# One second-stage matmul ahead of each convolution burst, and another order of the convolution's PSUM banks

## The chip, the cores and the metric

The kernel runs on one core of a Trainium2 chip. The metric is the device time of one execution in microseconds (us); lower is better. A core has a matrix engine (TensorE, PE in the profile, with PEld for its weight loads), a vector engine (VectorE, DVE), a scalar engine (ScalarE, ACT), GpSimd (POOL) and SyncE (SP), which here issues most DMAs. The engines run side by side and meet through semaphores. Matmul sums land in PSUM[...].

## The reference

Two steps follow each other. The first is a causal convolution over 7 positions with softmax weights, one set for each of 8 heads of 24 channels. The second is a feed-forward layer whose hidden value is the largest of three products.

```python
def _attn_ref(x, weight):                  # x: 8 x 4160 x 192, weight: 8 x 7
    w = softmax(weight, axis=-1)           # written out with exp and sum
    x_pad = np.concatenate([np.zeros((B, 6, D)), x], axis=1)
    idx = np.arange(S)[:, None] + np.arange(7)[None, :]
    x_unf = x_pad[:, idx, :].reshape(B, S, 7, 8, 24)
    return np.einsum('hk,bskhg->bshg', w, x_unf).reshape(B, S, D)

def _moe_ref(x, w1, w2, w3, w_out):        # x: 33280 x 192, w1..w3: 192 x 768, w_out: 768 x 192
    h = np.maximum(np.maximum(x @ w1, x @ w2), x @ w3)
    return h @ w_out
```

## The kernel before

**Blocks.** The 33280 tokens are cut into `NB` = 65 blocks of 512. Block t passes through three stages, in an order that the program writes out by hand: the loop `for t in range(2, NB)` issues, for each t, the first layer of block t, the second layer of block t-1, and in some turns the convolution of later blocks. Blocks 0 to 3 are convolved in another way (`conv_dense`) and play no part here.

**Convolution, a "burst".** `conv(u, pools)` (L301) issues 16 matmuls, 8 heads by two column halves, with 70 rows of `band` as weights. It writes tiles G into four PSUM banks, two heads each, and covers two blocks (u and u+1), except for block 4. It is issued right after `l1(t, 0)`: at t=3 for blocks 5 and 6, and at each even t from 4 to 60 for blocks t+3 and t+4. That makes 30 bursts of four banks; the one at t=2, for block 4 alone, uses two. `evac` (L347) copies a G bank to `ys`; `turn` (L358) and `double` (L366) then transpose and double it by DMAs from SP's queue into `yd`, the convolved block. `load_x` fetches x, and `cast_x` (L158) casts it on GpSimd.

**First layer.** `l1(t, j)` computes 128 of the 768 hidden values. The products are written as differences from the third: lp, for w1-w3, uses rows 0 to 63 of TensorE, the lower half; lq, for w2-w3, uses rows 64 to 127, the upper half. Each takes three matmuls of 512 columns, issued in turn, lp, lq, lp, lq, lp, lq (L399). ScalarE then makes `r` from lp (L403), and VectorE makes `h` from r and lq (L404). What was subtracted comes back in the second layer through the small matrix `m16`, which multiplies `yd`.

**Second layer.** `st2(t, u, NU)` issues one sixth of a block's second layer: five steps of two matmuls of 192 columns (L442), one in the lower half into tile po0 and one in the upper half into po1. The two halves keep sums of their own, and a pair of banks serves two of the block's four groups of 128 tokens. When both are complete, ScalarE copies po0 to `a` (L451), VectorE adds po1 to give `o` (L452), and `store` (L471) sends it out from GpSimd's queue.

**Order on TensorE.** For each j: six first-layer matmuls of block t, then ten second-layer matmuls of block t-1. At a burst, its 16 matmuls stand between `l1(t, 0)` and `st2(t-1, 0, NJ)`. This is the text of that stretch:

```python
        l1(t, 0)
        ...
        conv(u, PQ if t == 2 else WW + PQ)
        ...
        st2(t - 1, 0, NJ)
        for j in range(1, NJ):
            l1(t, j)
            st2(t - 1, j, NJ)
```

**PSUM banks.** Pool `psp` (tag p) has two banks for lp, `psq` (q) two for lq, and `psw` (w) four, which all po tiles share with two of a burst's G tiles. The other two G tiles take one bank of p and one of q. A pool hands out the bank that has been free longest, and the first matmul into it waits until the former tile has been read. As a burst takes one q bank, the lq of j=1 gets the bank of the lq of j=0, whose reader is h of j=0.

Of the kernel before, what the change touches and what calls it, by code (L numbers as in the profile page):

```python
# [27 lines left out]
def kernel(  # L28
# [19 lines left out]
    NJ = DFF // P  # L48
# [8 lines left out]
    for b in range(B):  # L57
        s = nfull * NBLK
        while s < SEQ:
            n = min(SEQ - s, NBLK - off)  # L60
# [8 lines left out]
    NB = len(blocks)  # L69
# [37 lines left out]
    psp = ctx.enter_context(tc.tile_pool(name="psp", bufs=2, space=bass.MemoryType.PSUM))  # L107
    psq = ctx.enter_context(tc.tile_pool(name="psq", bufs=2, space=bass.MemoryType.PSUM))
    psw = ctx.enter_context(tc.tile_pool(name="psw", bufs=4, space=bass.MemoryType.PSUM))
# [32 lines left out]
    def place(t):  # L142
        return (t, 0, 1) if t == NDENSE else (t - (t - NDENSE - 1) % 2, (t - NDENSE - 1) % 2, 2)
# [110 lines left out]
    def make_wd(j0, j1, eng=nc.vector):  # L254
        f = slice(P * j0, P * j1)
        eng.tensor_sub(out=wd[:, :, f], in0=ws[:, :, f], in1=w3s[:, :, f])  # L256
# [5 lines left out]
    def cast_w3(part):  # L262
        f = slice(PW * part, PW * (part + 1))
        nc.gpsimd.tensor_copy(out=w3h[:, :, f], in_=w3s[0:HALF, :, f])
# [24 lines left out]
    dense, hs, outs, halves, convs, done = {}, {}, {}, {}, {}, {}  # L289

    def conv(t, pools):
        if t >= NB:
            return
        t0, _, nu = place(t)
        n = len(pools)
        per = NHEAD // n
        w = nu * (NR // 2) * GRP
        G = [pool.tile([P, per, w], FP32, tag=tag, name=f"G{i}_{t}") for i, (pool, tag) in enumerate(pools)]
        for h in range(NHEAD):
            for c in range(2):  # L300
                nc.tensor.matmul(  # L301
                    G[h // per][HALF * c:HALF * (c + 1), h % per, :],
                    lhsT=band[0:HALF + PAD, h, PAD:HALF + PAD],
                    rhs=x16s[t0][0:HALF + PAD, h, c, :, :, :].rearrange("p u r c -> p (u r c)"),
                    start=True, stop=True, tile_position=(0, HALF * c))
        slots[t0] = ysp.tile([P, nu, NR // 2, D], FP16, tag="ys", name=f"ys_{t}")
        convs[t0] = G
# [75 lines left out]
    def y_tok(t, i, c, s):  # L383
        row = slice(HALF * i, HALF * (i + 1))
        if t < NDENSE:
            return dense[t][row, c, P * s:P * (s + 1)]
        k = spot(i, NC * s + c)
        return dense[t][row, k // (NCH // 2), k % (NCH // 2), :]
# [14 lines left out]
        nc.scalar.activation(out=r[:, 0:N], in_=ps[0][:, 0:N], func=AF.Relu)  # L403
        nc.vector.tensor_max(out=hs[t][:, j, 0:N], in0=r[:, 0:N], in1=ps[1][:, 0:N])  # L404

    def st2(t, u, NU):

        if t < 0:  # L410
            return
        hT = hs[t]
        if u == 0:
            todo = [[], []]
            for s in range(4):
                for i in range(2):
                    row = slice(HALF * i, HALF * (i + 1))
                    mm = [(y_tok(t, i, i, s), m16[row, 0, :])]
                    if s % 2 == i:
                        mm.append((y_tok(t, i, 2, s), m16[row, 1, :]))  # L420
                    hh = [(hT[row, j, P * s:P * (s + 1)], wo[row, j, :]) for j in range(NJ)]
                    mm = hh + mm if t == 0 else mm + hh
                    todo[i] += [(s, n == 0, n == len(mm) - 1, m) for n, m in enumerate(mm)]
            if t == NB - 1:

                for i in range(2):
                    k = [sum(e[0] < s for e in todo[i]) for s in range(5)]
                    lot = [todo[i][k[s]:k[s + 1]] for s in range(4)]
                    todo[i] = lot[0][:-1] + lot[1][:-1] + lot[0][-1:] + lot[1][-1:] + lot[2] + lot[3]
            halves[t] = (todo, {})  # L430
        todo, ps = halves[t]
        n = len(todo[0])
        for e in range(n * u // NU, n * (u + 1) // NU):
            for i in range(2):
                s, first, last, (a, b) = todo[i][e]
                b0 = s if t == NB - 1 else s - s % 2
                if (b0, i) not in ps:
                    pool, tag = (psw, "w")
                    if t == NB - 1 and s in (1, 2):
                        pool, tag = (psp, "p") if i == 0 else (psq, "q")  # L440
                    ps[b0, i] = pool.tile([P, 2, D], FP32, tag=tag, name=f"po{i}_{t}_{s}")
                nc.tensor.matmul(ps[b0, i][:, s % 2, :], lhsT=a, rhs=b, start=first, stop=last)  # L442
            ends = {todo[i][e][0] for i in range(2) if todo[i][e][2]}
            for s in sorted(ends):
                done[t, s] = done.get((t, s), 0) + sum(todo[i][e][0] == s and todo[i][e][2] for i in range(2))
                if done[t, s] < 2 or (s % 2 == 0 and t < NB - 1):
                    continue
                s0 = s if t == NB - 1 else s - 1
                ss = slice(s0 % 2, s % 2 + 1)
                a = tp.tile([P, 2, D], FP32, tag="a", name=f"a_{t}_{s}")  # L450
                nc.scalar.copy(out=a[:, ss, :], in_=ps[s0, 0][:, ss, :])  # L451
                nc.vector.tensor_add(out=outs[t][:, s0:s + 1, :], in0=a[:, ss, :],  # L452
                                     in1=ps[s0, 1][:, ss, :])
                if t == NB - 1 and s == 1:
                    store(t, 0, 2, (nc.sync,))
                elif t == NB - 1 and s == 3:
                    store(t, 2, 3, (nc.scalar,))
                    store(t, 3, 4, (nc.sync,))

    def store(t, s0, s1, qs):  # L460
        if t < 0:
            return
        ob, segs = outs[t], blocks[t]
        if len(segs) == 1:
            r = segs[0][0] * SEQ + segs[0][1] + P * s0
            todo = [(0, P, r, P)]
        else:
            assert all((b, S, n, off) == (b, SEQ - HALF, HALF, HALF * b) for b, S, n, off in segs)
            todo = [(HALF * i, HALF, (2 * s0 + i) * SEQ + SEQ - HALF, 2 * SEQ) for i in range(2)]
        for i, (p0, n, r, step) in enumerate(todo):  # L470
            qs[0].dma_start(out=bass.AP(tensor=out.tensor, offset=r * D,  # L471
                                        ap=[[D, n], [step * D, s1 - s0], [1, D]]),
                            in_=ob[p0:p0 + n, s0:s1, :])

    assert all(n == NBLK for n in blkN)
    def begin(t):
        hs[t] = hp.tile([P, NJ, NBLK], FP16, tag="h", name=f"h_{t}")
        outs[t] = outp.tile([P, 4, D], FP32, tag="o", name=f"o_{t}")


    PQ = ((psp, "p"), (psq, "q"))
    WW = ((psw, "w"), (psw, "w"))
    begin(0)
    begin(1)
    copy_w3(nc.vector.tensor_copy, 0)
# [16 lines left out]
    cast_w3(1)  # L502
    l1(1, 1, WW)
    transpose_w3(0)
# [4 lines left out]
    make_wd(4, 6, nc.gpsimd)  # L509
    l1(0, 3, WW)  # L510
    transpose_w3(2)
    l1(1, 2)
    l1(1, 3, WW)
    l1(0, 4)
    nc.gpsimd.tensor_copy(out=wo[:], in_=wos[:])
    l1(0, 5, WW)
    make_m(0)
# [17 lines left out]
    for t in range(2, NB):  # L535
        if t > 4:
            load_x(t + 6)
        for u in doubles_at.get(t, (t + 2,)):
            double(u)
        if t == 4:  # L540
            load_x(t + 6)
        if t > 3:
            cast_x(t + 5)
        begin(t)
        l1(t, 0)
        if t == 2:
            conv_dense(3, (nc.scalar.copy, nc.vector.tensor_copy, nc.scalar.copy))
            cross_dma(3)
            load_x(7)
        u = convs_at.get(t, t + 3 if t % 2 == 0 else NB)  # L550
        conv(u, PQ if t == 2 else WW + PQ)
        if t == 2:
            evac(u, 0)
            evac(u, 1, nc.vector.tensor_copy)
        else:
            for i in (0, 2):
                evac(u, i)
            for i in (3, 1):
                evac(u, i, nc.vector.tensor_copy)
        if t == 2:  # L560
            turn(4)
            load_x(8)
            cast_x(5)
            cast_x(6)
        elif t == 3:
            turn(5)
            turn(6)
            load_x(9)
            cast_x(7)
            cast_x(8)  # L570
        else:
            turn(t + 3)
# [4 lines that stand above are left out]
            if t == NB - 1 and j == 3:  # L577
                store(t - 1, 0, 2, (nc.sync,))
        if t == NB - 1:
            store(t - 1, 2, 4, (nc.sync,))  # L580
        else:
            store(t - 1, 0, 4, (nc.gpsimd,))
# [30 lines left out]
```

The softmax here doesn't subtract the row's maximum and nothing guards it: scores larger than these inputs give would overflow.

## Time and profile before

| what | value |
|---|---|
| median of 4 runs | 467.73 us (467.29 to 468.32) |
| the profiled execution | 467.5 us |
| its span in the profile | 465.7 us |
| TensorE busy, instructions | 459.9 us (99%), 7065 matmuls |
| VectorE, ScalarE, GpSimd busy | 359.0, 316.8, 162.5 us |
| one lp or lq matmul; one po; one G (mean as recorded) | 376, 243, about 250 ns |
| r; h; a; o (mean) | 597, 685, 471, 541 ns |

The span runs from the first to the last instruction that the profile shows; 1.8 us of the execution lie around it. A matmul's record has a start and a modelled end. Matmuls of one half follow each other more closely than the recorded durations, so the distance from start to start tells the pace. In the timeline each row gives the start and the duration in us, then engine, line, operation and tiles out<-in; "x16" means that 16 instructions are merged in the row. PEclk, the clock granted to TensorE, is full over the whole span.

### The profile page before, as it was taken

How to read it: one execution, taken by the hardware profiler on the slowest of the kernel's cores; microseconds unless marked ns; L12 is line 12 of the kernel's file. 1: busy time of each engine (PE TensorE's matmuls, PEld its weight loads, DVE VectorE, ACT ScalarE, POOL GpSimd, SP SyncE). 2: the span in 40 equal slices, each digit the busy share in tenths (PEclk: the TensorE clock that was granted, in tenths of full speed). 3: DMA queues.
4: the chain of work that ended last, by engine and by line, in shares of the span. 5: the costliest groups of instructions: out<-in, count | busy, mean ns of one | idle time of the engine just before them, and what ended most of it. 6: DMA issues, size and time to landing. Idle time of an engine off the chain costs nothing.

```text
span 465.7 us, 17191 instructions
## 1 busy us (share of the span) xinstructions
PE 459.9 (99%) x7065; PEld 386.1 (83%) x7065; DVE 359.0 (77%) x607; ACT 316.8 (68%) x609; POOL 162.5 (35%) x227
## 2 busy tenths in 40 slices
PE   8999999999999999999999999999999999999996
PEld 4587888888888888888888888988888898888996
DVE  6777877778777787787877777777778777777775
ACT  5766666666676766766667667676676666766664
POOL 5744434234324324433423432332343343243010
PEclk9999999999999999999999999999999999999999
DMA  8958997777678877979777867778686975794512
GB/s 199 236 133 203 207 230 170 170 202 168 182 187 167 185 183 178 177 170 208 186 138 202 170 186 181 191 166 182 180 173 165 210 191 146 187 164 108 118 69 103
DMA packets 107114, 81.14 MB, mean 174 GB/s; under 512 B 53110, under 2 KB 101980, under 8 KB 107036
## 3 DMA queue, kind: packets, MB, share of 16 engines
q1 hardware_dynamic: 99804, 55.17, 58.7%
q0 software_dynamic: 7072, 24.78, 14.8%
q8 instruction: 55, 0.90, 0.9%
q14 instruction: 23, 0.19, 0.1%
q10 hardware_dynamic: 160, 0.10, 0.1%
HBM read 30.28 MB, written 25.56 MB: 120 GB/s over the span
## 4 chain that ended last, share of the span: by engine, by line
PE 98%; DVE 0%; ACT 0%; issue 0%; DVEq 0%
PE lq L399 35%; PE po L442 33%; PE lp L399 22%; PE G L301 5%; PE idle L215 1%; PE D L319 1%; PE lw L399 0%; PE band_cols L239 0%; DVE wd L256 0%; PE pm L284 0%; PE pm L280 0%; ACT yd L328 0%; ACT yd L326 0%; ACT yd L325 0%; DVE h L404 0%
## 5 line engine op out<-in xcount | busy, mean ns | idle before, releaser
L404 DVE TENSOR_TENSOR h<-r,lq 128x512 f16<-128x512 f16 x386 | 264.6, 685 | 98.6 <-ACT r L403 98.5
L403 ACT ACTIVATE r<-lp 128x512 f16<-128x512 f32 x386 | 230.5, 597 | 136.8 <-PE lp L399 123.9
L399 PE MATMUL lp<-yd,wd 64*128 64x512 f16 x1158 | 312.1, 376 | 0.6 <-DVE wd L256 0.6
L399 PE MATMUL lq<-yd,wd 64*128 64x512 f16 x1158 | 312.2, 376 | 0.4 <-DVE yd L335 0.4
L442 PE MATMUL po<-wo,h 64*128 64x192 f16 x3120 | 249.0, 243 | 0.0
L442 PEld LDWEIGHTS <-h 64*128 64x128 f16 x3120 | 204.1, 94 | 16.8
L399 PEld LDWEIGHTS <-wd 64*128 64x128 f16 x2340 | 166.7, 94 | 28.0 <-issue 4.9
L471 POOL DMA_DIRECT2D out_dram<-o x64 | 48.1, 752 | 282.3 <-DVE o L452 215.9
L158 POOL CAST x<-xf 70x768 f16<-70x768 f32 x122 | 97.3, 832 | 3.3 <-DMA xf<-in_x_dram 2.9
L442 PE MATMUL po<-m,yd 64*128 64x192 f16 x780 | 95.8, 243 | 0.0
L452 DVE TENSOR_TENSOR o<-a,po 128x384 f32<-128x384 f32 (+1 forms) x132 | 71.3, 541 | 0.6 <-ACT a L451 0.6
L442 PEld LDWEIGHTS <-yd 64*128 64x128 f16 x780 | 58.0, 94 | 10.5
L451 ACT COPY a<-po 128x384 f32<-128x384 f32 (+1 forms) x132 | 62.0, 471 | 2.1 <-PE po L442 2.1
L347 DVE CAST ys<-G 128x384 f16<-128x384 f32 x61 | 31.0, 549 | 0.0
L301 PEld LDWEIGHTS <-band 70*64 70x64 f16 x496 | 19.5, 109 | 12.8 <-PE lp L399 12.7
L347 ACT CAST ys<-G 128x384 f16<-128x384 f32 x61 | 26.2, 486 | 0.0
L301 PE MATMUL G<-x,band 70*64 70x192 f16 (+1 forms) x496 | 26.1, 248 | 0.0
L215 PE MATMUL idle<-idle 128*128 128x512 f16 x15 | 6.3, 564 | 1.2 <-DVE idle L210 1.2
L177 POOL CAST xz<-xf 112x80 f16<-112x80 f32 (+2 forms) x18 | 5.2, 330 | 4.1 <-DMA xf<-in_x_dram 4.1
L319 PEld LDWEIGHTS <-xz 112*32 112x32 f16 x240 | 4.4, 105 | 1.9 <-DVE xz L177 0.8
L335 DVE COPY yd<-yd 64x512 f16<-64x512 f16 x9 | 4.2, 470 | 1.4 <-ACT yd L328 0.6
L319 PE MATMUL D<-band,xz 112*32 112x103 f16 (+1 forms) x240 | 5.0, 225 | 0.0
(45 smaller groups left out, 50.8 us busy)
## 6 DMA issues: line engine op xcount, KB each, us to landing
xf<-in_x_dram SPq DMA_DIRECT2D x57, 420.0 KB
out_dram<-o POOLq DMA_DIRECT2D x62, 384.0 KB, 3.7
yd<-yd SPq DMA_DIRECT2D x122, 96.0 KB
xf<-in_x_dram SPq DMA_DIRECT2D x7, 367.5 KB
ws<-in_moe_w_dram SPq DMA_DIRECT2D x6, 192.0 KB
yd<-ys SPq DMA_TRANSPOSE x61
w3s<-in_moe_w_dram SPq DMA_DIRECT2D x3, 192.0 KB
wos<-in_moe_w_out_dram SPq DMA_DIRECT2D x1, 576.0 KB
```

What stands on the lines that cost most here:

```text
L158: nc.gpsimd.tensor_copy(out=x16s[t0][0:K, :, c, u, :, :].rearrange("p h r c -> p r h c"), in_=xf[0:K, c:NR:2, :].rearrange("p r (h c) -> p ...
L215: nc.tensor.matmul(ps[:], lhsT=idle[:, 0:P], rhs=idle[:], start=True, stop=True)
L301: nc.tensor.matmul(G[h // per][HALF * c:HALF * (c + 1), h % per, :], lhsT=band[0:HALF + PAD, h, PAD:HALF + PAD], rhs=x16s[t0][0:HALF + PAD ...
L319: nc.tensor.matmul(ps[32 * g:32 * g + 32, lo:hi], lhsT=xz[t][v][0:rlen, q, 32 * s:32 * s + 32], rhs=band[0:rlen, h, cc:cc + hi - lo], star ...
L347: copy(out=slots[t][:, :, :, GRP * per * i:GRP * per * (i + 1)].rearrange("p u r (h c) -> p h (u r) c", c=GRP), in_=G[i][:].rearrange("p h ...
L399: nc.tensor.matmul(ps[i][:, 0:N], lhsT=wd[row, c, P * j:P * (j + 1)], rhs=y_all(t, i, c), start=(c == 0), stop=(c == NC - 1))
L403: nc.scalar.activation(out=r[:, 0:N], in_=ps[0][:, 0:N], func=AF.Relu)
L404: nc.vector.tensor_max(out=hs[t][:, j, 0:N], in0=r[:, 0:N], in1=ps[1][:, 0:N])
L442: nc.tensor.matmul(ps[b0, i][:, s % 2, :], lhsT=a, rhs=b, start=first, stop=last)
L451: nc.scalar.copy(out=a[:, ss, :], in_=ps[s0, 0][:, ss, :])
L452: nc.vector.tensor_add(out=outs[t][:, s0:s + 1, :], in0=a[:, ss, :], in1=ps[s0, 1][:, ss, :])
L471: qs[0].dma_start(out=bass.AP(tensor=out.tensor, offset=r * D, ap=[[D, n], [step * D, s1 - s0], [1, D]]), in_=ob[p0:p0 + n, s0:s1, :])
```

## The change

Ahead of each of the 30 bursts, one second-layer matmul is issued: the lower-half one of the first step of `st2(t-1, 0, NJ)`. It takes its po0 bank from `psw` before the burst takes its own. Behind the burst, `st2` leaves that one out (a set `ahead` remembers it), so the first second-layer matmul there is its upper-half partner; all others follow as before. The burst's four banks are filled in the order w, p, w, q instead of w, w, p, q. ScalarE evacuates the first w and then p, VectorE q and then the second w, as before; only the indices change.

```diff
-    def st2(t, u, NU):
+    ahead = set()
+
+    def st2(t, u, NU, first_half_only=False):
...
-        if u == 0:
+        if t not in halves:
...
-        for e in range(n * u // NU, n * (u + 1) // NU):
+        es = range(n * u // NU, n * (u + 1) // NU)
+        for e in es[:1] if first_half_only else es:
             for i in range(2):
+                if first_half_only:
+                    if i:
+                        break
+                    ahead.add((t, e))
+                elif i == 0 and (t, e) in ahead:
+                    continue
...
+    WPWQ = ((psw, "w"), (psp, "p"), (psw, "w"), (psq, "q"))
...
-        conv(u, PQ if t == 2 else WW + PQ)
+        if t > 2 and u < NB:
+            st2(t - 1, 0, NJ, True)
+        conv(u, PQ if t == 2 else WPWQ)
...
-            for i in (0, 2):
+            for i in (0, 1):
                 evac(u, i)
-            for i in (3, 1):
+            for i in (3, 2):
                 evac(u, i, nc.vector.tensor_copy)
```

## Prediction, made before the changed kernel was run

> **What bounds the kernel now.** The page first: one engine has no idle time, and the chain that ended last runs through it.
>
> ```profile
> PE 459.9 (99%) x7065; PEld 386.1 (83%) x7065; DVE 359.0 (77%) x607; ACT 316.8 (68%) x609; POOL 162.5 (35%) x227
> ...
> PE lq L399 35%; PE po L442 33%; PE lp L399 22%; PE G L301 5%; PE idle L215 1%; PE D L319 1%; PE lw L399 0%; PE band_cols L239 0%; DVE wd L256 0%; PE pm L284 0%; PE pm L280 0%; ACT yd L328 0%; ACT yd L326 0%; ACT yd L325 0%; DVE h L404 0%
> ```
>
> But TensorE is two streams: lp and the lower po run in rows 0 to 63, lq and the upper po in rows 64 to 127. "PE busy" hides a half that stands still while the other works, and so does the waits view, which lists no wait of a matmul on VectorE inside the loop. So I read next the timeline around a conv burst (G, L301), and took the starts to the nanosecond from the trace's records. First a burst that lq enters 0.10 us behind lp:
>
> ```profile
> 220.86 0.38 PE L399 MATMUL lp<-yd,wd 64*128 64x512 f16 x1
> 220.96 0.38 PE L399 MATMUL lq<-yd,wd 64*128 64x512 f16 x1
> ...
> 221.27 0.85 PE L301 MATMUL G<-x,band 70*64 70x192 f16 x16
> 221.28 0.60 ACT L403 ACTIVATE r<-lp 128x512 f16<-128x512 f32 x1
> 221.45 0.55 DVE L452 TENSOR_TENSOR o<-a,po 128x384 f32<-128x384 f32 x1
> ...
> 221.91 0.68 DVE L404 TENSOR_TENSOR h<-r,lq 128x512 f16<-128x512 f16 x1
> ...
> 222.05 0.34 PE L442 MATMUL po<-m,yd 64*128 64x192 f16 x3
> ...
> 222.48 0.38 PE L399 MATMUL lp<-yd,wd 64*128 64x512 f16 x1
> ...
> 222.65 0.37 PE L399 MATMUL lq<-yd,wd 64*128 64x512 f16 x1
> ```
>
> Then the burst before it, entered 0.17 us behind:
>
> ```profile
> 207.09 0.38 PE L399 MATMUL lp<-yd,wd 64*128 64x512 f16 x1
> 207.26 0.38 PE L399 MATMUL lq<-yd,wd 64*128 64x512 f16 x1
> 207.50 0.60 ACT L403 ACTIVATE r<-lp 128x512 f16<-128x512 f32 x1
> ...
> 207.57 0.85 PE L301 MATMUL G<-x,band 70*64 70x192 f16 x16
> ...
> 208.77 0.38 PE L399 MATMUL lp<-yd,wd 64*128 64x512 f16 x1
> 208.88 0.37 PE L399 MATMUL lq<-yd,wd 64*128 64x512 f16 x1
> ```
>
> Let Z be the start of the last lp matmul ahead of a burst and s the lag of lq behind lp. The 30 bursts from t=3 on agree within 4 ns: first G at Z+s+0.306; last G 0.605 later; first po 0.178 after that, so T = Z+s+1.089; five po per half (steps 0.093, then 0.0825), so lp of j=1 at T+0.424 = Z+s+1.513. The first lq of j=1 does not follow at once: it starts at **Z+1.785 in every burst, whatever s is**. Its bank is the one that h of j=0 reads. r starts at Z+0.413 and takes 0.597, h runs from Z+1.050 to Z+1.731, and lq follows 0.054 later. So on this path lq waits for lp, r, h, and the new lag is 1.785-1.513-s = 0.272-s. That is the alternation of the two fences: 0.098 gives 0.174, 0.172 gives 0.100 (the next group takes 0.003 off).
>
> From there to the next burst the upper half runs without a gap: 12.085 us in both kinds, eleven groups of 1.06 and the matmuls of the twelfth. One burst period is therefore (1.785-s)+12.085: **a larger lag on entering a burst is time saved, one for one**. The lags of the 29 bursts from t=4 on sum to 3.949, mean 0.136.
>
> **What the Trainium skill says.** "TensorE: Matmul & The Clock Gate", section "Back-to-back issue gap", gives N/2.4+2.5 ns: 215.8 for 512 columns and 82.5 for 192. The trace agrees: 0.216 between lp matmuls, 0.0825 between po. Its Part 3, "The mechanism", says that matmuls start and end strictly in program order. The trace disagrees between row halves: an lp starts at 220.432, ahead of the last po before it in the program, at 220.450. So the lower half may run ahead. "TensorEngine Tiling (Array Packing)", "Key Properties": a change of tiling mode drains the engine. The trace agrees: G starts 0.306 after the last lq, where the next matmul of that half would come after 0.216. "Perfetto Trace Analysis", "Tensor Engine Instruction", says matmul ends are modelled; I use starts only.
>
> **The change, part by part.** No instruction is added or removed. In 30 bursts (t=3 and every even t from 4 to 60) one lower po goes ahead of G, its upper partner stays first behind G.
>
> Ahead of G: the lower half is free at Z+0.216, and this po streams until Z+0.2985. The upper half streams until Z+s+0.216. With s above 0.083 the po lies under it and G does not move: cost nothing. It reads yd and m16, which are long there, not h; its bank's former sums, of the block before, were copied out some 3 us earlier.
>
> Behind G: the lower half has four po instead of five, so lp of j=1 comes at T+0.3415 = Z+s+1.431. lq stays at Z+1.785, since lp, r and h of j=0 do not move. The new lag is 0.354-s, less the 0.003: two lags in a row average 0.1755. Only half of the 0.0825 is gained, since the chain over r and h holds lq.
>
> Can the lag get that large? While lq waits, the weight load of the second lp is held behind it (in the first fence it is issued at 222.649, 2 ns after that lq). That lp is due 0.216 after the first, so about 0.21 is free. From 0.095 at t=3 the lags go 0.21, 0.14, 0.21: 15x0.21+14x0.1405 = 5.12. If they settle at once it is 29x0.1755 = 5.09. Gain 1.17 or 1.14 us.
>
> The end: the last block's po wait for h of its j=5, which follows from lp, not lq (the trace's lag falls to 0.005 at 460.58). lp is earlier than lq's gain says by the growth of the final lag, from 0.100 to 0.14 or 0.1755: 0.04 to 0.075 more. **Sum: 1.21 us.**
>
> The bank order w, p, w, q: nothing. ScalarE still copies the first w and then p; it has p's sums 0.165 earlier but is in the first copy (0.47 us). VectorE still takes q, then w, so the last evacuation stays, and with it the transposing DMA of SP behind it, the doubling DMAs, and POOL's stores and casts; none of these queues gets or loses an instruction. Waits that change place: the second G bank (p) waits for r of the block before (ended by Z-0.05, needed at Z+s+0.50); the third (w) for the copy a (ends Z+0.32, needed at Z+s+0.66); q as before. Covered also at s=0.095. The upper po now heads the queue behind G and waits for the add o (ends Z+1.134, seen 0.05 later: Z+1.184). With it late the lower po would stand behind it; it is in time when T is later, s above 0.095. At 0.14 the margin is 45 ns.
>
> Against its own time the profiled execution (467.5, span 465.7 and 1.8 around it) goes to 466.3. The median of four runs is 467.73, 0.2 above, so the forecast is 466.5.
>
> **Unknown costs.** (a) Where the drain is counted from, with a po as the last matmul ahead of G: from the end of both streams (G unmoved, which I take, since the trace counts it from the later half), or 0.306 after the po's own start, Z+0.522. (b) What a late weight load costs the second lp, c. Lower bound zero: the load at 222.649 was 0.043 ahead and cost nothing. Behind G loads come 4 ns ahead and the next step is 0.093 for 0.0825: c=0.01, which I take. Upper bound: the 0.094 that a load lasts. Earlier than due it cannot be, so no gain.
>
> **Rivals.** A, the drain follows the po: G at Z+0.522, lp of j=1 at Z+1.647, lag 0.1385 always, 0.135 at entry; 29x(0.136-0.135) is nothing, the tail gives 0.035: 467.7. For it: nothing here shows a short matmul ahead of G; against it: s+0.306 in both kinds.
> B, slower: the held weight load stalls the lower half at each burst. The lag is capped at 0.212-c; from c above 0.077 it falls under today's mean. The floor is 0.095 (at t=2 the lag is 0.003 on leaving and 0.095 six groups later), reached at c=0.12: 29x0.041 = 1.19 lost, 468.9. For it: the load is held in every burst; against it: the second lp came after 0.216 in all 30.
> C, the whole po is gained, 30x0.0825 = 2.5: 465.3. It needs lq free of h, and 1.785 in every burst speaks against it.
>
> **How the numbers follow.** About 0.2%, 0.94 us, is what a measurement here tells from no change. Main case 0.76 (own range 466.2 to 466.9), A 0.14, B 0.07, C 0.03. Faster by over 0.2%: 0.70 of the main case and C, 0.73; within 0.2%: 0.06 of the main case and A, 0.20; slower: B, 0.07. Range 466.0 to 467.8: it takes in the main case with the scatter of a median (runs 467.29 to 468.32) and A; B and C stay out.
>
> **What would show it.** Right: lq of j=1 still at Z+1.785; G at Z+s+0.306; lp of j=1 at Z+s+1.431; lags near 0.21 and 0.14 or all near 0.175; bursts 13.69 us apart on the mean (13.735 now). Wrong: lags of 0.1385 (A), under 0.13 with the second lp over 0.216 after the first (B), lq of j=1 before Z+1.7 (C), or a po that starts after the last lq has streamed.

## The result, and the profile after

The changed kernel takes **466.52 us** (median of 44 runs; 466.5 was forecast), the kernel before 467.76 us (median of 63). The ratio is 0.9968, 95% interval 0.9959 to 0.9977: faster, by about 0.3%. The ratio is one of means over the fast runs, so it leaves out two runs of the changed kernel, of 793 and 2650 us, and takes in nine runs of the kernel before near 471 us; the medians give 0.9973.

The page of the changed kernel shows almost none of it. Here are the busy times and the row of G's weight loads, whose last part is the idle time ahead of them (12.8 us before):

```profile
PE 459.4 (99%) x7065; PEld 370.9 (80%) x7065; DVE 359.1 (77%) x607; ACT 318.9 (69%) x609; POOL 162.6 (35%) x227
...
L301 PEld LDWEIGHTS <-band 70*64 70x64 f16 x496 | 19.5, 109 | 11.5 <-PE lp L399 11.4
```

TensorE's busy time is down by 0.5 us on the same 7065 matmuls, at 99% as before. The recorded time of the weight loads fell more, from 386.1; it goes with the lag of lq behind lp (400.1 us in e3 below, 357.0 in e4), and why it does is open. The span is only 0.7 us shorter, because in this execution the first of the 30 bursts comes 0.49 us later (Z at 35.38, not 34.89), before anything that the change touches; in another execution of the changed kernel, e8 below, it comes at 34.82. So the measure to use is the distance from the first burst to the last: **390.91 us, where it was 392.02**.

The timeline at two bursts in a row (start us, duration us, engine, line, operation, tiles); first one entered with a lag of 0.152 us, then one with 0.195:

```profile
56.42 0.38 PE L399 MATMUL lp<-yd,wd 64*128 64x512 f16 x1
56.57 0.38 PE L399 MATMUL lq<-yd,wd 64*128 64x512 f16 x1
56.63 0.24 PE L451 MATMUL po<-m,yd 64*128 64x192 f16 x1
...
56.88 0.85 PE L301 MATMUL G<-x,band 70*64 70x192 f16 x16
...
58.01 0.38 PE L399 MATMUL lp<-yd,wd 64*128 64x512 f16 x1
...
58.20 0.37 PE L399 MATMUL lq<-yd,wd 64*128 64x512 f16 x1
```

```profile
70.10 0.38 PE L399 MATMUL lp<-yd,wd 64*128 64x512 f16 x1
70.29 0.38 PE L399 MATMUL lq<-yd,wd 64*128 64x512 f16 x1
70.31 0.24 PE L451 MATMUL po<-m,yd 64*128 64x192 f16 x1
...
70.60 0.85 PE L301 MATMUL G<-x,band 70*64 70x192 f16 x16
...
71.15 0.68 DVE L404 TENSOR_TENSOR h<-r,lq 128x512 f16<-128x512 f16 x1
...
71.72 0.38 PE L399 MATMUL lp<-yd,wd 64*128 64x512 f16 x1
71.88 0.37 PE L399 MATMUL lq<-yd,wd 64*128 64x512 f16 x1
```

The new po starts 0.22 us after the last lp, and G follows the last lq by 0.31 as it always did: the po is hidden. From the last lp ahead of the burst (Z) to the first lq behind it there is still 1.78 us in both fences. What has changed is the lp behind the burst: to the nanosecond it comes 1.586 and 1.628 us after Z, where it was 1.612 and 1.682 in the two fences of the kernel before. So the lag, which went 0.10, 0.17, now goes 0.15, 0.20.

### The profile page after: what moved, and what is told of

Its sections match the earlier page's. It is cut to its first block, busy times and chain, and to the rows that moved or that the text cites. A ratio compares the mean times of both kernels' runs of the same rounds, so it can differ in the third digit from the quotient of the medians.

```text
span 465.0 us, 17191 instructions
## 1 busy us (share of the span) xinstructions
PE 459.4 (99%) x7065; PEld 370.9 (80%) x7065; DVE 359.1 (77%) x607; ACT 318.9 (69%) x609; POOL 162.6 (35%) x227
## 4 chain that ended last, share of the span: by engine, by line
PE 96%; DMA 1%; SPq 1%; DVE 0%; issue 0%; POOL 0%; ACT 0%; POOLq 0%
PE lq L399 38%; PE po L451 36%; PE lp L399 15%; PE G L301 6%; DMA xf<-in_x_dram 1%; PE D L319 1%; PE lw L399 0%; SPq L190 0%; POOL xz L177 0%; DVE wd L256 0%; DVE o L461 0%; SPq L134 0%; PE pm L284 0%; PE pm L280 0%; PE idle L215 0%
## 5 line engine op out<-in xcount | busy, mean ns | idle before, releaser
L451 PE MATMUL po<-wo,h 64*128 64x192 f16 x3120 | 263.3, 243 | 0.0
L451 PEld LDWEIGHTS <-h 64*128 64x128 f16 x3120 | 209.3, 94 | 20.9
L399 PEld LDWEIGHTS <-wd 64*128 64x128 f16 x2340 | 160.1, 94 | 37.4 <-issue 2.0
L451 PE MATMUL po<-m,yd 64*128 64x192 f16 x780 | 110.0, 243 | 0.0
L451 PEld LDWEIGHTS <-yd 64*128 64x128 f16 x780 | 62.4, 94 | 12.2
```

What stands on the lines that cost most here:

```text
L399: nc.tensor.matmul(ps[i][:, 0:N], lhsT=wd[row, c, P * j:P * (j + 1)], rhs=y_all(t, i, c), start=(c == 0), stop=(c == NC - 1))
```

## The experiments

All kernels are compared with the kernel before, run beside them (467.77 us beside e1 to e4, 467.60 beside e5 to e8). The ratio is estimated from the single runs and not from the medians, so it differs from the quotient of the medians by up to 0.002. "First to last" is the distance between the starts of the last lp ahead of the first and of the 30th burst, from the traces; "lag" is the mean of the 30 lags on entering a burst.

| kernel | median us | ratio (95% interval) | first to last, us | lag, us |
|---|---|---|---|---|
| before | 467.76 | | 392.02 | 0.135 |
| changed | 466.52 | 0.9968 (0.9959 to 0.9977) | 390.91 | 0.173 |
| e1, early po alone | 466.56 | 0.9958 (0.9940 to 0.9975) | 390.91 | 0.173 |
| e2, bank order alone | 467.61 | 0.9989 (0.9975 to 1.0002) | 392.02 | 0.135 |
| e3, upper half ahead | 468.93 | 1.0027 (1.0003 to 1.0051) | 393.29 | 0.095 |
| e4, two po ahead | 465.77 | 0.9941 (0.9916 to 0.9966) | 390.30 | 0.193 |
| e5, before with lq in w | 466.62 | 0.9987 (0.9973 to 1.0001) | 390.86 | 0.094 |
| e6, changed with lq in w | 464.12 | 0.9939 (0.9915 to 0.9962) | 388.77 | 0.093 |
| e7, two po ahead and lq in w | 463.81 | 0.9916 (0.9904 to 0.9929) | 388.33 | 0.156 |
| e8, changed once more | 466.53 | 0.9981 (0.9965 to 0.9998) | 390.91 | 0.173 |

**e1 and e2: the two parts of the change, each alone.**

```diff
# e1, against the changed kernel
-        conv(u, PQ if t == 2 else WPWQ)
+        conv(u, PQ if t == 2 else WW + PQ)
...
-            for i in (0, 1):
+            for i in (0, 2):
                 evac(u, i)
-            for i in (3, 2):
+            for i in (3, 1):
```

> The early lower-half matmul alone; the burst's banks in the old order w, w, p, q. Theory (the lag of lq behind lp is what is gained): the whole gain, 1.2 us off the time before (ratio 0.9974); lq of j=1 at Z+1.785, lp of j=1 at Z+s+1.43, mean lag on entering a burst 0.175. Rival (the new bank order spares a wait inside the burst): no gain, ratio 1.000.

```diff
# e2, against the kernel before
-        conv(u, PQ if t == 2 else WW + PQ)
+        conv(u, PQ if t == 2 else WPWQ)
...
-            for i in (0, 2):
+            for i in (0, 1):
                 evac(u, i)
-            for i in (3, 1):
+            for i in (3, 2):
```

> The bank order w, p, w, q alone, no matmul moved. Theory: nothing, ratio 1.000 within 0.0005; G's 16 starts still 0.605 us from first to last, lags 0.098 and 0.172 in turn. Rival (the order brings the gain): 1.2 us off, ratio 0.9974.

The early po alone gives the whole gain: 466.56 us, and the same 390.91 us from first burst to last as the changed kernel. The order alone leaves that distance at 392.02, to the hundredth; its interval includes 1. The order is worth nothing that these runs can show.

**e3: the other half goes ahead.** The same number of matmuls is moved, but into the half that ends last.

```diff
                 if first_half_only:
-                    if i:
-                        break
+                    if i == 0:
+                        continue
                     ahead.add((t, e))
-                elif i == 0 and (t, e) in ahead:
+                elif i == 1 and (t, e) in ahead:
                     continue
```

> As the changed kernel, but the matmul ahead of the burst is the upper-half one, and the lower-half one follows behind the burst. Theory: nothing covers it, so the first G starts at Z+s+0.389 in place of Z+s+0.306; lq of j=1 stays at Z+1.785 (it waits for h), lp of j=1 comes at Z+s+1.595, so the lag falls to its floor, 0.095, at every burst; 29 bursts x (0.136-0.095) = 1.2 us slower than before, ratio 1.0026. Rival (any second-layer matmul ahead of the burst shortens the stretch behind it, whichever half it is in): faster by about 1.2 us, ratio 0.9974.

Slower, 468.93 us; the interval lies wholly above 1. One burst of it in the timeline:

```profile
111.11 0.38 PE L399 MATMUL lp<-yd,wd 64*128 64x512 f16 x1
111.21 0.38 PE L399 MATMUL lq<-yd,wd 64*128 64x512 f16 x1
111.42 0.24 PE L451 MATMUL po<-m,yd 64*128 64x192 f16 x1
...
111.60 0.85 PE L301 MATMUL G<-x,band 70*64 70x192 f16 x16
...
112.80 0.38 PE L399 MATMUL lp<-yd,wd 64*128 64x512 f16 x1
112.90 0.37 PE L399 MATMUL lq<-yd,wd 64*128 64x512 f16 x1
```

The po comes after the last lq of its half, and G 0.39 us after that lq in place of 0.31. lq behind the burst is at Z+1.79 again. But lp has come so late that the lag is at its floor, 0.095 on the mean of all bursts. It is the lag that costs, not the later G: the time from Z to the first lq has not moved.

**e4: two matmuls ahead.**

```diff
-        for e in es[:1] if first_half_only else es:
+        for e in es[:2] if first_half_only else es:
```

> As the changed kernel, with two lower-half matmuls ahead of the burst, their two upper partners behind it. Theory: they stream until Z+0.381, the upper half until Z+s+0.216, so at a lag of 0.2 they still lie nearly under it; G near Z+0.51, lp of j=1 near Z+1.555, raw lag 0.23, which the held weight load of the second lp cuts to about 0.197 (the second lp comes a little over 0.216 after the first); 29x(0.197-0.136) = 1.77 and 0.1 at the end, 1.9 us off the time before, ratio 0.9960. Rival 1 (the drain ahead of G runs from the last po's own start): G at Z+0.60, lag 0.14, ratio 0.9997. Rival 2 (matmuls of the two halves keep the program's order behind the burst, so the third lower po waits for the second upper one): lp of j=1 0.09 later, lag 0.14, ratio 0.9997.

465.77 us, 0.75 under the changed kernel, as the theory gave (465.9), and 1.72 us less than before from first to last burst (1.77 was expected). The timeline, with the two po merged in one row:

```profile
110.92 0.38 PE L399 MATMUL lp<-yd,wd 64*128 64x512 f16 x1
111.11 0.38 PE L399 MATMUL lq<-yd,wd 64*128 64x512 f16 x1
111.13 0.33 PE L451 MATMUL po<-m,yd 64*128 64x192 f16 x2
...
111.42 0.85 PE L301 MATMUL G<-x,band 70*64 70x192 f16 x16
...
112.47 0.38 PE L399 MATMUL lp<-yd,wd 64*128 64x512 f16 x1
112.54 0.24 PE L451 MATMUL po<-wo,h 64*128 64x192 f16 x1
112.70 0.37 PE L399 MATMUL lq<-yd,wd 64*128 64x512 f16 x1
112.71 0.39 PE L399 MATMUL lp<-yd,wd 64*128 64x512 f16 x1
```

Three readings. G still follows the last lq by 0.31, so rival 1 is out. The lp at 112.47 runs ahead of a po at 112.54 that stands before it in the program, and it comes at Z+1.55, not at Z+1.64, so rival 2 is out. And the cap on the lag, the weight load of the second lp that is held behind lq, is at work: lq is held until 112.70, and the second lp comes at 112.71, 0.241 us after the first in place of 0.216. The raw lag of 0.235 enters the next burst as 0.196.

**e5 to e7: lq is taken off h's bank.** If h of j=0 is what holds lq at Z+1.785, lq should be free in another bank.

```diff
+    LW = ((psp, "p"), (psw, "w"))
...
-            l1(t, j)
+            l1(t, j, LW if j == 1 and t > 2 and u < NB else PQ)
```

e5 is this edit on the kernel before, e6 on the changed kernel, e7 on e4.

> The kernel before, with the lq of j=1 behind each of the 30 bursts in a w bank (the burst's first G bank, which ScalarE has emptied by Z+1.43) in place of the q bank that h of j=0 reads. Theory (lq of j=1 is held by h): it now starts when TensorE reaches it, Z+s+1.51, together with lp; the lag leaves the burst near 0 and climbs back to its floor of 0.095 in the following groups, at the upper half's cost. 30x(1.649-1.509-0.095) = 1.4 us off the time before, ratio 0.9971. Rival (h is not what holds lq; the stretch behind a burst is set by the drain and the matmuls alone): no change, ratio 1.000.

> The changed kernel with the same bank for the lq of j=1. Theory: lq at Z+s+1.51, lp at Z+s+1.43, lag 0.08 on leaving the burst and 0.095 at the next, so the upper half loses only 0.017 on the way; 3.4 us off the time before, ratio 0.9927, more than twice the gain of the changed kernel. Rival: as the changed kernel, ratio 0.9974.

> Two lower-half matmuls ahead of the burst and the lq of j=1 in a w bank. Theory: the lag settles where both po just fit under the last lq, near 0.16, above the floor; G at Z+0.47, lq of j=1 at Z+1.67, burst period 1.516+12.085; 4.0 us off the time before, ratio 0.9913. Rival: as with two matmuls ahead alone, 465.8, ratio 0.9957.

One burst of e6, where the lq of j=1 shows as lw:

```profile
110.30 0.38 PE L399 MATMUL lp<-yd,wd 64*128 64x512 f16 x1
110.39 0.38 PE L399 MATMUL lq<-yd,wd 64*128 64x512 f16 x1
110.51 0.24 PE L451 MATMUL po<-m,yd 64*128 64x192 f16 x1
110.69 0.85 PE L301 MATMUL G<-x,band 70*64 70x192 f16 x16
...
111.35 0.68 DVE L404 TENSOR_TENSOR h<-r,lq 128x512 f16<-128x512 f16 x1
...
111.83 0.38 PE L399 MATMUL lp<-yd,wd 64*128 64x512 f16 x1
111.90 0.38 PE L399 MATMUL lw<-yd,wd 64*128 64x512 f16 x1
```

lw starts at Z+1.607, while h still runs (111.35 to 112.03): h was the holder. With the early po the gain grows from 1.24 to about 3.5 us (464.12 against 467.60 beside it). Without it, in e5, it is 1.0 us by the medians and 1.16 us from first burst to last; the interval of its ratio just reaches 1.0001. 1.4 was expected, 0.045 per burst, and the trace has 0.041. lq stands at Z+s+1.515, 0.006 later than expected, and the climb of the lag back to its floor costs 0.093, about the 0.095 that was counted.

The climb also points to what the floor is. lp and lq leave the burst 0.003 apart and stay so for three groups; in the fourth, lq is held. Behind the burst at 110.61, the last lp of j=2, the h of j=2 and the first matmuls of j=4:

```profile
113.70 0.38 PE L399 MATMUL lp<-yd,wd 64*128 64x512 f16 x1
...
114.75 0.69 DVE L404 TENSOR_TENSOR h<-r,lq 128x512 f16<-128x512 f16 x1 [0.37 <-ACT r L403]
...
115.39 0.38 PE L399 MATMUL lp<-yd,wd 64*128 64x512 f16 x1
115.48 0.37 PE L399 MATMUL lq<-yd,wd 64*128 64x512 f16 x1
```

With two q banks, the lq of j=4 gets the bank of the lq of j=2. The h that reads that bank ends at 115.432, and lq starts 0.053 later, the distance seen behind a burst (0.054). By its timing, then, **the floor is the same wait for h, two groups apart**: lq comes 1.784 after the last lp of two groups earlier, lp comes 1.688 after it, and 0.096 lies between. In e3, e5 and e6, which run at the floor, the median distance from the end of that h to lq is 0.053 us; in the changed kernel, e4 and e7, whose lags are larger, it is never under 0.108 once the first burst is past. A third q bank, which would test it, was not tried.

With lq free of h behind the burst, it no longer holds that a larger lag on entering it is time saved. The period is then what the lower half needs: lp of j=1 at Z+s+1.440 and 12.092 from there to the next Z, which with a lag s of 0.093 makes the 13.625 us that e6 takes. A smaller lag would now be better, and the floor stands in the way.

e7 keeps the lag at 0.158 or 0.159 in every group from the first burst on, clear of the floor and of the cap. Its two po end at Z+0.381, later than the last lq, so lp of j=1 stands at Z+1.519 and not at a distance from s, and the bursts are 13.610 apart. At **463.81 us it is the fastest kernel of the study** (5 runs; e6 has 6), 3.8 us under the kernel before beside it; from first burst to last it is 0.43 us ahead of e6.

**e8: the changed kernel once more, beside e5 to e7.**

> The changed kernel as it is, on the same chip as the three others. All theories: 466.5, ratio 0.9974.

466.53 us, and 390.91 us from first burst to last for the third time.

## Why the prediction was right, step by step

- **What bounds.** The upper half and its wait for h: right. Z+1.785 holds in all 30 bursts of the changed kernel (1.783 to 1.787). e6 shows the cause, by taking the wait away.
- **The early po costs nothing.** Right: G at Z+s+0.305 to 0.306 in every burst. Rival A, with G at Z+0.522, is out: G came at Z+0.400 to Z+0.503. "TensorEngine Tiling (Array Packing)", "Key Properties", says that a mode change drains the engine, and not from when. The first burst of e4 tells: with a lag of 0.092 its two po end last, at Z+0.381 by their starts and the 0.0825 step, and G comes at Z+0.470. That is 0.09 behind the later of the two streams, as in all other bursts (0.306-0.216), and as in the bursts of e7, where the two po end last too (0.471-0.381). The upper po behind G and its wait for the add o came out as feared at a small lag: at the first burst, with a lag of 0.095, the first po started at Z+1.186 and lp of j=1 was 0.005 late; at 0.152 and more nothing of it is seen.
- **Only half of the po is gained.** Right: lp of j=1 at Z+s+1.433 (1.431 predicted), new lag 0.352-s (0.354 predicted). The lags of the 29 bursts from t=4 on sum to 5.08, mean 0.1752; 5.09 to 5.12 was predicted, and 3.95 is what the kernel before has. That makes 1.13 us; 1.11 is measured between the bursts, as lq of j=1 and the next burst each came some 0.0004 us later on the mean. (The prediction's 12.085 from that lq to the next burst is 12.088 in both traces, so full periods are 13.700 us and were 13.739; it gave 13.69 and 13.735.) Rival C, the whole po, needs lq free of h, which e6 had to arrange.
- **The end.** From the 30th Z to the start of the last copy a there is 35.12 us, where it was 35.19: 0.07 us, within 0.04 to 0.075. By the lags, 1.13 and 0.07 make 1.20, against 1.21; by the clock of the traces, 1.18; by the medians of all runs, 1.24. That the median lands within 0.02 us of the forecast is in part luck, as the runs scatter over more than that.
- **The held weight load.** The price c was taken as 0.01. At the first burst, with a raw lag of 0.252, the second lp started 0.006 behind the held lq, 0.042 later than due. The lag entered the next burst at 0.197, not 0.21, so some 0.013 more went in the matmuls behind it. In rival B's terms, a cap of 0.212-c, c is 0.015: near the lower bound, and far from the 0.077 from which rival B decides. e3 shows what B's floor costs: 1.2 us, as worked out for it. What the floor is, the prediction left open: by the timing in e5 it is the same wait for h.
- **The lags' course.** Predicted 0.21 and 0.14 in turn; seen 0.197 and 0.152 at first. In both traces of the changed kernel they drift together (to 0.180 and 0.171 at the end, in e8 to 0.185 and 0.166); in e1, with the old bank order, they stay at 0.198 and 0.151. The mean is the same, as the sum of two lags is fixed. Whether the bank order or chance makes them drift is open.
- **The bank order.** Nothing in time, as e2 shows.
- **The skill on matmul order.** "TensorE: Matmul & The Clock Gate", Part 3, "The mechanism", has matmuls start and end strictly in program order. In every trace here the two row halves depart from it, in e4 by at least one po. A lag above one po step, 0.0825, means that a lower po starts ahead of an upper one that precedes it, so the gain depends on it.

## What to carry to other kernels

Where two halves of TensorE run side by side, take the matmul starts of each half apart: a busy share of 99% can hide a half that waits for a bank, and here the waits view doesn't list it. Work moved into a half's idle stretch pays only up to the next wait that both halves hang on, so look for that wait first; here another bank for one matmul brought about as much alone as the move (e5: 1.16 us from first burst to last, against 1.11), and 2.14 us more on top of it (e6). And ask of a lag or a floor that looks fixed which reader of a bank it stands for: the floor here goes, by its timing, with the two banks that take turns. Judge small gains by the distance between two marks in the trace that lie behind the start-up: here it was the same to 0.01 us in three traces of the same order of matmuls on TensorE, while the start-up ahead of it differed by up to 0.6 us between executions.

## What the runs showed of the hardware that was not expected

The drain ahead of a change of tile shape counts from the later half's last column (its last start and one step, 0.216 or 0.0825 us), not from the last matmul issued: G starts 0.09 us after it where lq ends last (the changed kernel) and where po does (e7). An lq that waits for h also holds the weight loads behind it for the lower half: at the first burst of the changed kernel the load starts 2 ns after the held lq, and the second lp 6 ns after it. In e4 the lower half runs 0.197 us, over two po, ahead of the upper one from burst to burst, at the same 1.06 us per group.
